# The last twenty entries of a hand-written emission list in another order, and one store moved behind them

## The chip, the cores and the metric

The kernel runs on one core of one Trainium2 chip. The metric is the device time of one execution in microseconds (us). The core has a matrix engine (TensorE, PE in the profile), which multiplies from on-chip memory (SBUF) into accumulators (PSUM), a vector engine (VectorE, DVE), an activation engine (ScalarE, ACT), a general engine (GpSimd, POOL), and SyncE (SP), which here issues nearly all DMA transfers, one after the other, from a queue of its own. Each engine works through its own list of instructions in order. An instruction that waits holds up everything behind it on that engine, and on SP that means the transfers behind it are not issued.

## The reference, cut to what matters

Three stages follow each other. The first is a delta-rule attention over 768 positions, the second a layer with a squared ReLU, the third a gated layer. The change touches the end of the second stage (called the first layer below) and the beginning of the preparation of the third (the second layer).

```python
def _moe_ref(x, w_in, w_out):            # x: 3072 x 384, w_in: 384 x 2048, w_out: 2048 x 384
    h = np.maximum(x @ w_in, 0.0)
    return (h * h @ w_out).astype(np.float32)

def _moe2_ref(x, w_gate, w_val, w_out):  # 384 -> 1536 -> 384
    gate = 1.0 / (1.0 + np.exp(-(x @ w_gate)))
    val = x @ w_val
    return (gate * val @ w_out).astype(np.float32)
```

The weights arrive as 64-bit numbers. The kernel turns them into 32-bit floats itself and keeps each as a high part and a low part, so that every product of the reference becomes three matrix multiplications (high with high, low with high, high with low).

## The kernel before, in words

The 3072 tokens are worked in six groups of 512 (`GT`), and the hidden width of the first layer in 16 slices of 128 (`NF1`). Piece n = 16 g + f, from 0 to 95, is slice f of group g. For each piece PE does nine multiplications for the hidden values (`h,n`, L677), and later nine for the output (`o,n`, L715), which add up in three PSUM tiles over the 16 slices of a group. Between the two, ACT takes the ReLU (L691) and squares it twice (L693, L694), and DVE makes the low part `gl` (`g,n`, L700). The hidden values live in two PSUM tiles (`ps_h`, tag `h`), so `h,n` cannot begin before the ReLU of `h,n-2` has been read.

The high parts of the weights stay in SBUF. The low parts are fetched from DRAM for each piece by SP at L655: `li,n` fetches the part that `h,n` needs, `lw,n` the part that `o,n` needs, each 192 KB, each into a ring of three tiles. All tiles of both rings have the name `il` in the profile.

The order of all this is written out by hand. `ORDER` is a list of entries such as `h,80` or `lw,82`, and the kernel emits the instructions of each entry in the order of the list (`run`, and `fns` for what a name stands for). The list ends with `h,81`. A loop then emits the remaining pieces in a regular pattern, one step for each piece n from 82 on: `h,n`, `li,n+2`, `lw,n+1`, `o,n-2`, `g,n`, and what `plan` holds for the step. So the first products behind the list are those of `h,82`, `o,80`, `h,83`, `o,81`. `plan` (filled by `at_step`) prepares the second layer: it loads the first layer's result back (`load_x2`, L887, at steps 1 and 2), converts the last third of the second layer's weights (`w2_late`, L786 to L807), and splits weights and inputs.

The first two thirds of the second layer's weights are converted within the list, in twelve chunks. `w2,i,k` is step k of chunk i: 0 fetches 768 KB (`raw`, L137, SP), 1 scales on ACT (L143), 2 and 3 are two DVE instructions each (L148 and L152, L157 and L161), 4 adds on POOL (L168), and 5 stores 384 KB to DRAM (`w2d`, L231, SP). Chunk 11 is the last.

Other entries in the stretch: `k2,5,1` fetches keys for the attention (L307, 384 KB in runs of 48 floats); of its possible readers, `s_piece` returns at once for group 5, half 1, so nothing reads this one. `x,5,1` splits the attention's result (L125 on ACT, L126 on DVE). `o,79` is the last piece of group 4, and ends with two copies on ACT (L726, L727) and one on DVE (L728); `po,4` stores them (L733, L734, SP).

```python
    with tc.manual_schedule():
        for token in ORDER.split():
            run(token)
```

Of the kernel before, what the change touches and what calls it, by code (L numbers as in the profile page):

```python
# [84 lines left out]
p,5,1 li,75 lw,73 lw,72 w,5,1 o,72 o,73 lw,74 g,74 v,5,1 w2,9,1 w2,9,2 sv,5,1 w2,9,3 s,5,0 li,78 h,75 z,5,0 g,75  # L85
w2,9,4 w2,9,5 h,76 g,76 o,74 ks,5,1 o,75 w2,10,0 w2,10,1 h,78 lw,76 x,5,0 li,77 t,5,1 o,76 h,77 g,77 y,5,1 li,82
li,79 lw,78 h,79 lw,77 lw,79 o,77 g,78 li,81 w2,10,2 z,5,1 w2,10,3 g,79 li,80 x,5,1 w2,10,4 w2,10,5 w2,11,0
w2,11,1 w2,11,2 w2,11,3 w2,11,4 k2,5,1 o,78 o,79 lw,82 h,80 lw,81 h,81 w2,11,5 g,80 li,83 po,4 g,81 lw,80
"""

@with_exitstack
def kernel(
# [132 lines left out]
    w2_todo = []  # L225
# [427 lines left out]
    def fetch_low(n, i):  # L653
        t = ring.tile([128, DM], F32R, tag=("il", "ol")[i], name="il", bufs=3)
        nc.sync.dma_start(out=t.bitcast(F32), in_=w1d[:, n % NF1, i])  # L655
        w1c[i, n] = t
# [10 lines left out]
    def moe1_hm(n, lo, hi_):  # L667
        g = n // NF1
        cs = slice(lo, hi_)
        if lo == 0:  # L670
            h_tile(n)
        hi, lo = w1h[n % NF1], w1c[0, n]
        xh, xl = xhi_t[g], xlo_t[g]
        ps = h_ps[n]
        for i, (w, x) in enumerate([(hi, xh), (lo, xh), (hi, xl)]):
            for kc in range(KD):
                nc.tensor.matmul(  # L677
                    out=ps[:, cs], lhsT=w[:, kc * 128:kc * 128 + 128], rhs=x[:, kc, cs],
                    start=(i == 0 and kc == 0), stop=(i == 2 and kc == KD - 1),
                )  # L680
# [22 lines left out]
    po = [None] * KD  # L703
# [35 lines left out]
    def keep_warm(n):  # L739
# [14 lines left out]
        k2=load_k2, kz=load_z, be=lambda: nc.sync.dma_start(out=beta_t, in_=beta), cs=constants, sq=squares, sm=sums, no=norms,  # L754
# [6 lines left out]
        w2=lambda i, k: w2_todo[i][k](), z=y_rows, po=put_x2,  # L761
        li=lambda n: fetch_low(n, 0), lw=lambda n: fetch_low(n, 1), h=moe1_h, h0=lambda n: moe1_hm(n, 0, GT // 2),
# [7 lines left out]
    with tc.manual_schedule():  # L770
# [115 lines left out]
        def load_x2(g):  # L886
            nc.sync.dma_start(out=x2r_t[:, g % 2], in_=x2d[g])  # L887
# [52 lines left out]
        def at_step(n, *fns):  # L940
            plan.setdefault(n, []).extend(fns)

        at_step(1, lambda: load_x2(0))
        at_step(2, lambda: load_x2(1))
        for m in range(NW):
# [348 lines left out]
```

## Time and profile before

| | us |
|---|---|
| median of three runs | 1089.73 (1089.73 to 1089.91) |
| the profiled execution, its own time | 1089.84 |
| its span (first to last instruction) | 1088.1 |
| PE busy | 1013.5 (93%) |
| DVE busy | 765.8 (70%) |
| ACT busy | 462.5 (43%) |
| POOL busy | 200.1 (18%) |
| longest wait of PE on a transfer (L715 for `il`) | 6.4 |

PE is busy for 93% of the span, and the chain of work that ended last runs through PE for 84% of it. So a wait of PE is what to look for, and what such a wait costs is read in the stretch where it stands. A row of the timeline gives the start and the duration of an instruction, or of several equal ones together, and in brackets how long its engine had been idle and for what. The durations of matrix multiplications overlap, so the distance from one start to the next is the measure of PE's pace.

### The profile page before, as it was taken

To read this page: it belongs to the slowest core of one execution; us is meant where nothing else is said; L and a number is where in the kernel's file an instruction comes from. 1 tells how busy PE (TensorE), PEld (TensorE's weight loads), DVE (VectorE), ACT (ScalarE), POOL (GpSimd) and SP (SyncE) were. 2 spreads that over 40 slices of the span, in tenths; PEclk is the share of its full clock that TensorE was granted. 3 is DMA by queue.
4 is the path that set the end of the run, shared out by engine and by line. 5 is a ranking of instruction groups with operands and counts; after the bars stand their busy time and mean duration, and the time that the engine had idled before them with its cause. 6 is when DMAs were issued, how large, how long until landed. Compare 5 with 4: busy or idle time off the path is not lost.

```text
span 1088.1 us, 27387 instructions
## 1 busy us (share of the span) xinstructions
PE 1013.5 (93%) x11611; PEld 830.8 (76%) x11611; DVE 765.8 (70%) x1450; ACT 462.5 (43%) x762; POOL 200.1 (18%) x157
## 2 busy tenths in 40 slices
PE   3476999999998999999996999999999999999998
PEld 2475778877887888888785887777888888878878
DVE  6779879868777776875342498888776665686770
ACT  2253765454454455445543574434332232233220
POOL 4342444100001101010010122335401221000000
PEclk9998999999999999999998999999999999999999
DMA  9766756775685956575545867553545323244302
GB/s 241 198 198 177 223 180 196 217 205 147 175 201 163 234 164 206 168 176 166 144 151 164 277 187 277 189 198 117 189 156 160 106 93 125 87 128 154 125 3 57
DMA packets 104843, 182.78 MB, mean 168 GB/s; under 512 B 46608, under 2 KB 79504, under 8 KB 100112
## 3 DMA queue, kind: packets, MB, share of 16 engines
q1 hardware_dynamic: 104432, 180.76, 55.7%
q8 instruction: 91, 1.49, 0.6%
q10 hardware_dynamic: 288, 0.26, 0.1%
q14 instruction: 32, 0.26, 0.1%
HBM read 139.30 MB, written 36.96 MB: 162 GB/s over the span
## 4 chain that ended last, share of the span: by engine, by line
PE 84%; DVE 8%; issue 4%; DMA 2%; ACT 1%; POOL 1%; SPq 1%; DVEq 0%; ACTq 0%; POOLq 0%
PE o L715 18%; PE h L677 18%; PE gx L1135 11%; PE gy L1135 11%; PE o L1014 10%; PE r L1194 2%; PE att L594 2%; PE att L536 1%; PE att L551 1%; PE att L582 1%; PE att L363 1%; PE att L616 1%; PE att L564 1%; PE att L377 1%; PE att L618 1%
## 5 line engine op out<-in xcount | busy, mean ns | idle before, releaser
L700 DVE TENSOR_TENSOR gl<-gg,gh 128x512 fp32r<-128x512 f32 x96 | 73.8, 776 | 106.6 <-ACT gg L694 106.5
L691 ACT ACTIVATE gg<-h 128x512 f32<-128x512 f32 x96 | 57.5, 598 | 190.0 <-PE h L677 181.2
L715 PE MATMUL o<-gh,il 128*128 128x512 f32 x288 | 113.9, 395 | 6.4 <-DMA il<-w1d 6.4
L1014 PE MATMUL o<-gh,wo 128*128 128x512 f32 x270 | 93.0, 394 | 0.0
L715 PE MATMUL o<-gh,w1h 128*128 128x512 f32 x216 | 88.1, 408 | 0.0
L715 PE MATMUL o<-gl,w1h 128*128 128x512 f32 x216 | 85.5, 396 | 0.0
L677 PE MATMUL h<-xhi,il 128*128 128x512 f32 x288 | 82.6, 395 | 0.9 <-issue 0.8
L1135 PE MATMUL gx<-xa,wg 128*128 128x512 f32 x288 | 76.7, 395 | 2.1 <-DVE valB L1047 1.2
L1135 PE MATMUL gy<-xa,wg 128*128 128x512 f32 x288 | 76.2, 393 | 0.0
L715 PEld LDWEIGHTS o<-gh,il 128*128 128x128 f32 x288 | 54.9, 191 | 17.5 <-DMA il<-w1d 6.8
L677 PE MATMUL h<-xhi,w1h 128*128 128x512 f32 x216 | 65.6, 413 | 1.8 <-ACT gg L691 1.8
L1135 PEld LDWEIGHTS gx<-xa,wg 128*128 128x128 f32 x288 | 53.6, 188 | 16.4 <-DVE gateB L1047 2.3
L677 PEld LDWEIGHTS h<-xhi,il 128*128 128x128 f32 x288 | 54.8, 191 | 13.7 <-issue 1.0
L1135 PEld LDWEIGHTS gy<-xa,wg 128*128 128x128 f32 x288 | 53.7, 188 | 13.0 <-DVE gateC L1047 0.4
L694 ACT ACTIVATE gg<-gg 128x512 f32<-128x512 f32 x96 | 60.7, 632 | 3.1
L693 ACT ACTIVATE gh<-gg 128x512 fp32r<-128x512 f32 x96 | 60.7, 632 | 3.1
L677 PE MATMUL h<-xlo,w1h 128*128 128x512 f32 x216 | 61.9, 396 | 0.0
L1014 PEld LDWEIGHTS o<-gh,wo 128*128 128x128 f32 x270 | 50.7, 188 | 11.9
L168 POOL TENSOR_TENSOR y<-raw 128x768 f32<-128x768 f32 x12 | 18.8, 1566 | 216.6 <-DVE raw L161 184.7
L1014 PE MATMUL o<-gl,wo 128*128 128x512 f32 x135 | 53.2, 394 | 0.0
L461 DVE TENSOR_TENSOR tmp<-xi,tt 128x40 f32<-128x40 f32 (+7 forms) x208 | 52.2, 284 | 1.2
L468 DVE TENSOR_TENSOR tt<-tt,tmp 128x40 f32<-128x40 f32 (+7 forms) x208 | 50.5, 276 | 1.4
(228 smaller groups left out, 2264.5 us busy)
## 6 DMA issues: line engine op xcount, KB each, us to landing
il<-w1d SPq DMA_DIRECT2D x192, 192.0 KB, 3.7
wg<-wgd SPq DMA_DIRECT2D x24, 1152.0 KB, 5.2
raw<-in_w_dram SPq DMA_DIRECT2D x19, 768.0 KB, 5.1
wgd<-wg SPq DMA_DIRECT2D x12, 1152.0 KB, 6.0
w1s<-in_w_dram SPq DMA_DIRECT2D x9, 768.0 KB, 5.3
w1d<-wl SPq DMA_DIRECT2D x16, 384.0 KB, 4.0
kz<-in_kz_dram SPq DMA_DIRECT2D x32, 192.0 KB, 5.1
kn<-in_kn_dram SPq DMA_DIRECT2D x12, 384.0 KB, 4.6
```

The source lines that it names most:

```text
L461: nc.vector.tensor_tensor(out=tv[i], in0=xi[:, 0:j, j].unsqueeze(2).to_broadcast([128, j, n]), in1=tt[:, j, lo:hi].unsqueeze(1).to_broadca ...
L468: nc.vector.tensor_tensor(out=tt[:, 0:j, lo:hi], in0=tt[:, 0:j, lo:hi], in1=tv[i], op=ALU.subtract)
L594: nc.tensor.matmul(out=psv[c][tok(a), k, :], lhsT=k2_t[st][tok(a), 8 * c + k, :], rhs=u_t[st][tok(a), 8 * c + k, 0:HD], start=True, stop=True,
L677: nc.tensor.matmul(out=ps[:, cs], lhsT=w[:, kc * 128:kc * 128 + 128], rhs=x[:, kc, cs], start=(i == 0 and kc == 0), stop=(i == 2 and kc == ...
L691: nc.scalar.activation(out=gg, in_=ps, func=ACTF.Relu)
L693: nc.scalar.activation(out=gh, in_=gg, func=ACTF.Square)
L694: nc.scalar.activation(out=gg, in_=gg, func=ACTF.Square)
L700: nc.vector.tensor_tensor(out=gl, in0=gg, in1=gh.bitcast(F32), op=ALU.subtract)
L715: nc.tensor.matmul(out=po[m], lhsT=w[:, cs], rhs=x, start=(f == 0 and i == 0), stop=(f == NF1 - 1 and i == 2),)
L1014: nc.tensor.matmul(out=po2[g, m], lhsT=w, rhs=x, start=start, stop=stop)
L1135: nc.tensor.matmul(out=ps, lhsT=a, rhs=c, start=k == 0 and u == us[0], stop=k == 2 and u == us[-1],)
L1194: nc.tensor.matmul(out=po_m, lhsT=x[:, cs], rhs=w, start=f == 0 and i == 0, stop=f == NF2 - 1 and i == 2)
```

## The change

The last twenty entries of the list stand in another order, and one of them, `w2,11,5` (the store of the last chunk), has left the list: it is issued in step 2 of the loop, before the second load of the first layer's result. Nothing is computed in another way.

```diff
@@ -85,7 +85,7 @@
 li,79 lw,78 h,79 lw,77 lw,79 o,77 g,78 li,81 w2,10,2 z,5,1 w2,10,3 g,79 li,80 x,5,1 w2,10,4 w2,10,5 w2,11,0
-w2,11,1 w2,11,2 w2,11,3 w2,11,4 k2,5,1 o,78 o,79 lw,82 h,80 lw,81 h,81 w2,11,5 g,80 li,83 po,4 g,81 lw,80
+lw,80 o,78 lw,81 o,79 k2,5,1 h,80 lw,82 h,81 g,80 li,83 w2,11,1 w2,11,2 g,81 w2,11,3 w2,11,4 po,4
 """
@@ -940,6 +940,7 @@
         def at_step(n, *fns):
             plan.setdefault(n, []).extend(fns)
 
+        at_step(2, lambda: w2_todo[11][5]())
         at_step(1, lambda: load_x2(0))
         at_step(2, lambda: load_x2(1))
```

PE's own order is the same in both kernels. On SP, before, from the fetch of the last chunk (`raw`) on; `il_8434` is `lw,82`, `il_8451` is `lw,81`, `il_8471` is `li,83`, `il_8477` is `lw,80`:

```order
L137 DMA raw_8401<-in_w2_dram 128x1536
L307 DMA k21_119<-in_ks_dram 128x16x48
L655 DMA il_8434<-w1d_105 128x384
L655 DMA il_8451<-w1d_105 128x384
L231 DMA w2d_106<-y_8404 128x768
L655 DMA il_8471<-w1d_105 128x384
L733 DMA x2d4_70<-o01_8429 128x1024
L734 DMA x2d4_70<-o2_8430 128x512
L655 DMA il_8477<-w1d_105 128x384
```

The same place on SP after the change; here `il_8403` is `lw,80`, `il_8414` is `lw,81`, `il_8446` is `lw,82`, `il_8465` is `li,83`:

```order
L137 DMA raw_8401<-in_w2_dram 128x1536
L655 DMA il_8403<-w1d_105 128x384
L655 DMA il_8414<-w1d_105 128x384
L307 DMA k21_119<-in_ks_dram 128x16x48
L655 DMA il_8446<-w1d_105 128x384
L655 DMA il_8465<-w1d_105 128x384
L733 DMA x2d4_70<-o01_8425 128x1024
L734 DMA x2d4_70<-o2_8426 128x512
```

`lw,80` has moved from behind the store and `po,4` to the place right behind the fetch of `raw`, and the store (L231) is gone from here. On SP it stands now further down, in the loop, between the fetches of `li,86` and `lw,85` (`il_8570`, `il_8572`) and the second load of the first layer's result (`x2d1`):

```order
L887 DMA x2r_8486<-x2d0_66 128x1536
L655 DMA il_8570<-w1d_105 128x384
L655 DMA il_8572<-w1d_105 128x384
L231 DMA w2d_106<-y_8468 128x768
L887 DMA x2r_8486<-x2d1_67 128x1536
L786 DMA raw2_8488<-in_w2_dram 128x768
```

On ACT, before, from the split of the attention's result on (the three rows from L691 are the ReLU and the squares of `h,80`, the next of `h,81`):

```order
L125 CAST xhi<-xr 128x3x256
L143 ACTIVATE raw<-raw 128x768
L726 COPY o_8429<-o_7360 128x512
L727 COPY o_8429<-o_7361 128x512
L691 ACTIVATE gg<-h 128x512
L693 ACTIVATE gh<-gg 128x512
L694 ACTIVATE gg<-gg 128x512
```

And after the change:

```order
L125 CAST xhi<-xr 128x3x256
L726 COPY o_8425<-o_7360 128x512
L727 COPY o_8425<-o_7361 128x512
L691 ACTIVATE gg<-h 128x512
L693 ACTIVATE gh<-gg 128x512
L694 ACTIVATE gg<-gg 128x512
L691 ACTIVATE gg<-h 128x512
L693 ACTIVATE gh<-gg 128x512
L694 ACTIVATE gg<-gg 128x512
L143 ACTIVATE raw<-raw 128x768
```

The scaling of the chunk (L143), which waits for the fetch of `raw`, has moved from ahead of the copies and of the ReLUs of `h,80` and `h,81` to behind them.

## Rows read from the trace of the kernel before

**Rows 1.** Page, first line: the span.
```profile
span 1088.1 us, 27387 instructions
```
**Rows 2.** Timeline of PE, 573 to 610: start, duration, instruction, count, idle before.
```profile
573.50 0.84 PE L677 MATMUL h<-xhi,w1h 128*128 128x512 f32 x3
575.54 0.84 PE L677 MATMUL h<-xhi,w1h 128*128 128x512 f32 x3
...
579.50 0.97 PE L677 MATMUL h<-xhi,w1h 128*128 128x512 f32 x3 [1.76 <-ACT gg L691]
...
581.68 0.39 PE L715 MATMUL o<-gh,w1h 128*128 128x512 f32 x1
588.48 0.79 PE L715 MATMUL o<-gh,il 128*128 128x512 f32 x1 [6.41 <-DMA il<-w1d]
...
594.84 0.40 PE L715 MATMUL o<-gh,w1h 128*128 128x512 f32 x1
...
609.14 0.84 PE L677 MATMUL h<-xhi,w1h 128*128 128x512 f32 x3
```
**Rows 3.** Windows: stretch, length, busy us of five engines, clock, DMA share, GB/s.
```profile
579.50:581.68 2.18, 2.18 (x10) 1.80 (x10) 2.11 (x4) 2.12 (x4) 0.37 (x1) 1.00 0.03 11
581.68:588.48 6.80, 0.39 (x3) 0.01 (x1) 2.94 (x4) 2.74 (x5) 1.09 (x1) 0.87 0.72 256
588.48:592.05 3.57, 3.57 (x8) 2.80 (x9) 0.00 (x0) 0.00 (x0) 0.00 (x0) 0.50 0.02 8
```
**Rows 4.** Timeline of SP's queue, 572 to 603: start, time to issue, transfer.
```profile
572.01 0.38 SPq L137 DMA_DIRECT2D raw<-in_w_dram  x1
572.44 0.55 SPq L307 DMA_DIRECT2D k<-in_ks_dram  x1
573.08 3.74 SPq L655 DMA_DIRECT2D il<-w1d  x1
...
582.80 0.32 SPq L231 DMA_DIRECT2D w2d<-y  x1
...
584.72 1.01 SPq L655 DMA_DIRECT2D il<-w1d  x1
...
601.31 0.43 SPq L887 DMA_DIRECT2D x2r<-x2d  x1
...
602.26 0.43 SPq L655 DMA_DIRECT2D il<-w1d  x1
```
**Rows 5.** DMA issues at 572.01, 572.44, 573.08, 584.72, 602.26: size, us to landing.
```profile
raw<-in_w_dram SPq DMA_DIRECT2D x1, 768.0 KB, 5.0
k<-in_ks_dram SPq DMA_DIRECT2D x1, 384.0 KB, 6.9
...
il<-w1d SPq DMA_DIRECT2D x1, 192.0 KB, 6.8
...
il<-w1d SPq DMA_DIRECT2D x1, 192.0 KB, 3.7
...
il<-w1d SPq DMA_DIRECT2D x1, 192.0 KB, 5.4
```
**Rows 6.** Timeline of ACT, 577 to 579.
```profile
577.12 0.88 ACT L143 ACTIVATE raw<-raw 128x768 f32<-128x768 f32 x1 [4.72 <-DMA raw<-in_w_dram]
...
578.84 0.61 ACT L691 ACTIVATE gg<-h 128x512 f32<-128x512 f32 x1
```
**Rows 7.** Instructions on tile raw, 560 to 590: duration ns min/median/max.
```profile
L148 DVE TENSOR_SCALAR y<-raw x2: 554/558/562, 566.5 to 578.0; 128x768 uint32<-128x768 uint32 x2
...
L161 DVE SCALAR_TENSOR_TENSOR raw<-raw,y x2: 959/960/960, 568.6 to 580.2; 128x768 f32<-128x768 uint32 x2
L168 POOL TENSOR_TENSOR y<-raw x2: 1467/1652/1837, 569.7 to 581.3; 128x768 f32<-128x768 f32 x2
```
**Rows 8.** Waits of PE, 594 to the end: total us, times, longest.
```profile
PE gx L1135 <- DVE valC L1047: 1.6, 1, 1.6
```

## The prediction

> **What bounds the kernel now.** I read the page first, then PE's own timeline around the changed entries, then what released its waits (SP's queue, the landings of its transfers, ACT), and last the granted clock of the same stretch. The profiled execution took 1089.84 us, 1.74 more than its span [rows 1] and 0.11 more than the median of the runs.
>
> PE should be followed from `h,80` on, where the changed entries begin to matter. `h,80` starts at 573.50 and `h,81` at 575.54 [rows 2], so a piece of nine multiplications takes 2.04 us at full pace, 0.227 each. `h,82` would follow at 577.58, but starts at 579.50: it needs the PSUM tile of `h,80`, and ACT reads that only at 578.84, because it had first waited for the fetch of `raw` until 577.12 and then scaled it and made two copies [rows 6]. `o,80` begins at 581.68 and stops after one product: the second, which needs `lw,80`, comes at 588.48 after 6.41 us of idleness [rows 2]. `lw,80` is the transfer issued at 584.72 [rows 4], landing 3.7 later at 588.4 [rows 5]. It was issued so late because the store of the last chunk stood before it on SP, and that was issued at 582.80 only [rows 4], when POOL had finished the chunk. The chain is thus: fetch of `raw`, ACT, four DVE instructions, POOL, store, and only then a weight that PE needs at once.
>
> [...] `o,81` starts at 594.84 [rows 2].
>
> **What the change takes away.** `lw,80` moves ahead of the store, and the store leaves this place; L143 moves behind the activations of `h,80` and `h,81`. PE's order does not change. From 573.50 to 594.84 there are 21.34 us with five pieces (`h,80`, `h,81`, `h,82`, `o,80`, `h,83`), 45 products, which at full pace take 5 x 2.04 = 10.20. The 11.14 us between are, by the starts in [rows 2]:
> - `h,82` late, 579.50 - 577.58 = 1.92;
> - its own piece, 2.18 instead of 2.04: 0.14;
> - `o,80` between its first and second product, 6.80 instead of 0.23: 6.57;
> - the 17 products from 588.48 to 594.84, 6.36 instead of 17 x 0.227 = 3.86: 2.50, the price of the slow clock.
>
> Sum 11.13. If nothing new is late, `h,82` starts at 577.58, `o,80` at 579.62, `h,83` at 581.66, `o,81` at 583.70, and all that follows on PE comes 11.1 us earlier.
>
> [...] The rows show 0.50 after the idle time, and 1.00 in 579.50 to 581.68, after the shorter wait of 1.76 [rows 2, 3]. [...]
>
> **What could be late next, step by step.**
> - `lw,80` is needed by the second product of `o,80`, at 579.85. It is now issued where the keys were, at 572.44 [rows 4]. The fetch of `raw` ahead of it lands at 572.01 + 5.0 = 577.0. A 192 KB part lands 0.5 behind its predecessor when the queue is full: `k` at 572.44 + 6.9 = 579.3, the `il` behind it at 573.08 + 6.8 = 579.9 [rows 4, 5]. So `lw,80` lands at 577.5, and cannot be later than the 579.9 of that `il`, which had both ahead of it: the cost lies between 0 and 0.1. I take 0.
> - `lw,81` follows 0.5 later, at 578.0, and is needed at 583.9.
> - `li,83` is needed by the fourth product of `h,83`, at 581.66 + 0.68 = 582.3. Ahead of it now stand `raw`, `lw,80`, `lw,81`, `k` and `lw,82`. `k` took 2.3 behind `raw` (577.0 to 579.3), so 577.0 + 2 x 0.5 + 2.3 + 2 x 0.5 = 581.3. SP must also get to issue it. Behind `k`, the issue of one `il` took 3.74, to 576.82 [rows 4], 2.5 before `k` landed; with `k` 1.0 later this ends at 577.8, and `li,83` is issued at about 577.9, 3.4 before the landing worked out. The margin is 1.0, the smallest here. Cost between 0 and, if SP were held until `k` has landed (580.3) and the transfer then took the 3.7 of the one at 584.72 [rows 5], 584.4 - 582.3 = 2.1. I take 0, since the only row of this situation says so.
> - ACT: the copies no longer wait for `raw`, so the ReLU of `h,80` is at 575.7 and its PSUM tile free at 576.3, before 577.58. L143 now comes behind six activations of about 0.6 [rows 6], at 579.7, when `raw` has long landed, and ends at 580.6. The ReLU of `h,82`, ready at 579.8, is 0.8 late; its result is wanted by `o,82` at 587.8. Hidden by two pieces and more.
> - DVE: `gl` of piece 81 now stands behind L148 and L152. From 580.6: 0.56 [rows 7], another of 0.96 like L161 [rows 7], and a `gl` of some 0.7 give 582.9; `o,81` wants it with its third product, at 584.2. Margin 1.3, cost 0; without that cover each us of delay on ACT is one of PE.
> - POOL and the store: the remaining two DVE instructions end at 584.4, POOL adds up to 1.84 [rows 7]: 586.2. SP comes to the store just before the second load of the first layer's result, which it issued at 601.31 [rows 4], now at 601.31 - 11.1 = 590.2. No wait, by 4 us. It costs SP some 0.4 and the queue 384 KB, at the pace of the `il` (192 KB in 0.5) 1.0. Behind it stands `li,87`: issued at 602.26, landed 5.4 later at 607.7 [rows 4, 5], needed by the fourth product of `h,87`, at 609.14 + 0.68 = 609.8 [rows 2]. Of the 2.1 us 0.7 to 1.1 remain. Cost 0; with the store at half that pace (2.0 and 0.4) 0.3.
>
> So the sum is -11.1: 1089.84 - 11.1 = 1078.7, and against the median, which lies 0.11 below, 1078.6. Downstream PE waits only for DVE's part of the second layer [rows 8], which follows PE itself; I let 1.0 to either side stand for these handovers, less than the longest of them.
>
> **The rivals.**
> 1. *The wait moves to the next fetch* (`li,83` at `h,83`, or `li,87` behind the store). For it: the margins of 1.0 and 0.7; 3.74 us for an issue behind `k`. Against it: the same row, carried over, still leaves the margin. Price: up to 2.1 for `li,83` and 0.3 for `li,87`, and half a us for a restart like those 0.14; no slow clock, as after the 1.76 [rows 3]. Together 1079.2 to 1081.3. Chance 0.2.
> 2. *The clock does not come back*: the terms of waiting go (8.6), the 2.50 stay. For it: 0.87 was already granted within the stretch with the wait [rows 3]. Against: 1.00 before it. 1089.73 - 8.6 = 1081.1. Chance 0.04.
> 3. *The change doesn't do what it says*: `lw,80` is emitted before `o,78`, and if its tile came free only behind `o,79` and the landing slipped again behind other transfers, the hole at `o,80` would stay. Against: `lw,82` stood in that very place and was issued at 573.08 [rows 4]. Time 1089.7, if all of it stayed. Chance 0.03.
> 4. *Slower*: the store as a plug on SP. In the loop every fetch of PE stands behind it. If POOL finished the chunk late, SP would hold `x2d1`'s load, the second layer's first slab and `li,87` together. It decides from POOL's end at 590.2 + 0.7 = 590.9 on; to eat 11.1 us, of which 2.5 would be a slow clock again, POOL would have to end near 599.5, and 3 us later the time is 1092.7. For it: that queue did just this at 582.80. Against: POOL's end at 586.2 by the rows. Chance 0.02.
>
> **How the numbers follow.** The forecast has 0.71. Its own range is 1077.6 to 1079.6 by the handovers. The range goes to 1077.2 below and 1081.6 above, which takes in rivals 1 and 2 and leaves out 3, 4 and a forecast that is off for a reason not listed here. A measurement can tell 0.2%, 2.2 us, from no change; the forecast and rivals 1 and 2 are faster by more, 0.95, of which I give 0.01 away to what is not listed; no change 0.03; slower 0.03.
>
> **What the profile after would show.** Right: no idle time of PE before L677 or L715 between `h,80` and `o,81`, the granted clock at 1.00 through the whole stretch, nine products every 2.04; the `il` behind `raw` landing about 0.5 after it; L143 without idle time before it; the store's issue without a wait, just before the second load. Wrong: an idle time of PE for `il` at the fourth product of a piece of `h` (rival 1), 0.50 in the clock without a wait before it (rival 2), a hole after the first product of `o,80` (rival 3), SP's queue waiting for POOL at L231 in the loop (rival 4). A span under 1075 would mean that something behind `o,81` gained too.

## The result and the profile after

The changed kernel took 1077.71 us (median of 4 runs, 1074.27 to 1079.54) beside 1089.82 for the kernel before: ratio 0.988, 95% interval 0.985 to 0.9911. In a second series it took 1075.98 (6 runs) beside 1088.0 (29 runs, 1083.02 to 1095.11): 0.9888, 0.9856 to 0.9921. The first median lies 0.9 below the forecast. The second lies below the range, and so does 0.988 x 1089.73 = 1076.7. The profiled execution took 1074.27; the first line of its page, which answers to [rows 1]:

```profile
span 1072.5 us, 27390 instructions
```

PE's timeline of the changed kernel, from `h,80` to `o,81` and at `h,87`, answers to [rows 2]:

```profile
568.39 0.84 PE L677 MATMUL h<-xhi,w1h 128*128 128x512 f32 x3
...
570.43 0.84 PE L677 MATMUL h<-xhi,w1h 128*128 128x512 f32 x3
...
572.48 0.84 PE L677 MATMUL h<-xhi,w1h 128*128 128x512 f32 x3
...
574.51 0.39 PE L715 MATMUL o<-gh,w1h 128*128 128x512 f32 x1
574.74 0.39 PE L715 MATMUL o<-gh,il 128*128 128x512 f32 x1
...
576.55 0.84 PE L677 MATMUL h<-xhi,w1h 128*128 128x512 f32 x3
...
578.60 0.39 PE L715 MATMUL o<-gh,w1h 128*128 128x512 f32 x1
...
592.88 0.84 PE L677 MATMUL h<-xhi,w1h 128*128 128x512 f32 x3
594.12 0.96 PE L677 MATMUL h<-xhi,il 128*128 128x512 f32 x3 [0.41 <-DMA il<-w1d]
```

Three things are to be seen. The pieces follow each other every 2.04 us; the wait ahead of `h,82` and the hole behind the first product of `o,80` are gone, and `h,80` to `o,81` takes 578.60 - 568.39 = 10.21 instead of 21.34. A new wait stands at `h,87`: its `il` products come 1.24 behind its start instead of 0.68. And `h,80` itself starts 5.1 us earlier than before, although PE's instructions ahead of it are the same and the order on the other engines differs only within the last 1.5 us before it.

The windows of the changed kernel (stretch, length, busy us of PE, PEld, DVE, ACT and POOL, clock, DMA share, GB/s) show a clock of 1.00 from `h,80` to `h,87`, where [rows 3] had 0.50 from 588.48 to 592.05:

```profile
568.39:578.60 10.21, 10.21 (x47) 8.45 (x46) 4.51 (x7) 6.37 (x11) 0.00 (x0) 1.00 1.07 313
578.60:592.88 14.28, 14.28 (x65) 11.83 (x64) 3.17 (x5) 7.37 (x12) 1.79 (x1) 1.00 0.74 259
```

SP's queue of the changed kernel (start, time to issue, transfer), beside [rows 4]:

```profile
566.90 0.38 SPq L137 DMA_DIRECT2D raw<-in_w_dram  x1
567.38 0.48 SPq L655 DMA_DIRECT2D il<-w1d  x1
...
568.95 4.06 SPq L655 DMA_DIRECT2D il<-w1d  x1
573.12 0.37 SPq L655 DMA_DIRECT2D il<-w1d  x1
...
585.10 0.38 SPq L231 DMA_DIRECT2D w2d<-y  x1
585.53 0.42 SPq L887 DMA_DIRECT2D x2r<-x2d  x1
...
586.64 0.51 SPq L655 DMA_DIRECT2D il<-w1d  x1
```

The landings of those issued at 566.90 (`raw`), 567.38 (`lw,80`), 573.12 (`li,83`), 585.53 (the second load of the first layer's result) and 586.64 (`li,87`), with size and us to landing, beside [rows 5]:

```profile
raw<-in_w_dram SPq DMA_DIRECT2D x1, 768.0 KB, 5.2
...
il<-w1d SPq DMA_DIRECT2D x1, 192.0 KB, 5.3
...
il<-w1d SPq DMA_DIRECT2D x1, 192.0 KB, 3.4
...
x2r<-x2d SPq DMA_DIRECT2D x1, 768.0 KB, 7.1
...
il<-w1d SPq DMA_DIRECT2D x1, 192.0 KB, 7.4
```

`raw` lands at 572.1. `lw,80` lands at 572.7 and is needed at 574.74. `li,83` lands at 576.5 and is needed at 576.55 + 0.68 = 577.23. `li,87` lands at 594.1 and is needed at 593.56: that is the new wait. The store at 585.10 did not wait for POOL, whose last addition begins at 579.17 and takes 1.79; L143 on ACT has no idle time before it any more, in contrast to [rows 6]:

```profile
579.17 1.79 POOL L168 TENSOR_TENSOR y<-raw 128x768 f32<-128x768 f32 x1 [12.71 <-DVE raw L161]
```

```profile
574.51 0.87 ACT L143 ACTIVATE raw<-raw 128x768 f32<-128x768 f32 x1
```

PE's waits from 568 to the end, the groups of `gx` by valC (the same as in [rows 8], one line lower in the file) and of `h`:

```profile
PE gx L1136 <- DVE valC L1048: 1.6, 1, 1.6
...
PE h L677 <- DMA il<-w1d: 0.4, 1, 0.4
```

So one execution can be cut at three marks: the start of `h,80`, `o,81`, and the first `gx` product. From there to the end every kernel here took 438.0 to 438.2. The table gives the marks of one profile of each kernel. Its last columns are the ratio that follows from the two middle stretches alone (their sum against the 76.44 of before, over 1088), and the measured one:

```
kernel                 h,80    h,80-o,81  o,81-gx  by the marks  measured
before                 573.50  21.34      55.10
before, repeated       573.34  21.27      55.08    0.9999        1.0008 [0.9979, 1.0037]
changed                568.39  10.21      55.78    0.9904        0.988  [0.985, 0.9911]
changed, repeated      566.31  10.20      55.82    0.9904        0.9888 [0.9856, 0.9921]
lw,80 early only       567.06  14.19      55.09    0.9934        0.994  [0.9914, 0.9966]
conversion late only   574.67  23.54      55.08    1.0020        1.0035 [1.0008, 1.0062]
store in the list      575.77  10.20      63.02    0.9970        0.9975 [0.9952, 0.9998]
before, PE kept busy   569.82  19.00      55.08    0.9978        0.9979 [0.9949, 1.0009]
store at step 9        568.53  10.20      55.08    0.9897        0.9885 [0.9855, 0.9916]
the same without k2    569.73  10.20      55.08    0.9897        0.9897 [0.9863, 0.9931]
```

Each ratio worked out from the marks lies in the measured interval. The gain of the change is 10.4 to 10.5 us, 11.1 in the list less 0.7 at `h,87`. The start of `h,80`, with the same instructions of PE ahead of it in every kernel, scatters over 9.5 us.

### The profile page after: what moved, and what is told of

It reads as the page before. It is cut to its first block, busy times and chain, and to the rows that moved or that the text cites. A ratio compares the mean times of both kernels' runs of the same rounds, so it can differ in the third digit from the quotient of the medians.

```text
span 1072.5 us, 27390 instructions
## 1 busy us (share of the span) xinstructions
PE 1008.8 (94%) x11611; PEld 828.3 (77%) x11611; DVE 763.4 (71%) x1450; ACT 462.4 (43%) x762; POOL 201.4 (19%) x157
## 4 chain that ended last, share of the span: by engine, by line
PE 85%; DVE 7%; issue 3%; DMA 2%; ACT 1%; SPq 1%; POOL 1%; DVEq 0%; ACTq 0%; POOLq 0%
PE h L677 18%; PE o L715 18%; PE gx L1136 12%; PE gy L1136 11%; PE o L1015 10%; PE r L1195 2%; PE att L594 2%; PE att L536 1%; PE att L363 1%; PE att L551 1%; PE att L582 1%; PE att L616 1%; PE att L564 1%; DMA il<-w1d 1%; PE att L618 1%
## 5 line engine op out<-in xcount | busy, mean ns | idle before, releaser
L700 DVE TENSOR_TENSOR gl<-gg,gh 128x512 fp32r<-128x512 f32 x96 | 70.3, 738 | 96.4 <-ACT gg L694 96.2
L691 ACT ACTIVATE gg<-h 128x512 f32<-128x512 f32 x96 | 57.4, 598 | 185.7 <-PE h L677 175.1
L715 PEld LDWEIGHTS o<-gh,il 128*128 128x128 f32 x288 | 54.1, 188 | 10.5
L168 POOL TENSOR_TENSOR y<-raw 128x768 f32<-128x768 f32 x12 | 19.1, 1593 | 221.0 <-DVE raw L161 221.0
```

Source lines behind the costliest of these rows:

```text
L691: nc.scalar.activation(out=gg, in_=ps, func=ACTF.Relu)
L700: nc.vector.tensor_tensor(out=gl, in0=gg, in1=gh.bitcast(F32), op=ALU.subtract)
L715: nc.tensor.matmul(out=po[m], lhsT=w[:, cs], rhs=x, start=(f == 0 and i == 0), stop=(f == NF1 - 1 and i == 2),)
```

## The experiments

**The two kernels again.** No edit.

> The kernel before once more, unchanged. Marks are read from PE's timeline: the start of h,80 (573.50 in the first trace of before, 568.39 in that of the changed kernel, though every instruction ahead of it is the same in both), and the distance from there to the start of o,81 (21.34 and 10.21). Theory A: the 5.1 us by which the changed kernel reached h,80 earlier are scatter of the first 150 us (attention start-up), which differs from execution to execution; then this second trace of the same program may reach h,80 anywhere from 568 to 575, and its times scatter by some 3 to 5 us around 1089. Theory B: the lead belongs to the changed program; then this one reaches h,80 at 573.5 within 0.5 and its times stay within 1 us of 1089.8. Both: 21.3 from h,80 to o,81.

> The changed kernel once more, unchanged. Theory A (start-up scatter): h,80 starts anywhere from 568 to 575, the times spread from 1074 to 1080 and sit 10.6 below those of before on average (11.1 from h,80 to o,81, less the 0.6 that h,87 now waits for li,87). Theory B (the lead belongs to the program): h,80 at 568.4 within 0.5, median near 1074.5. Both: 10.2 from h,80 to o,81, and a wait of h,87 for il of 0.3 to 0.7.

Measured: 1088.62 (12 runs, 1081.7 to 1096.8) and 1075.98 (6 runs, 1072.25 to 1077.6). The middle stretches repeat to 0.1 us. The three runs of before that lay within 0.18 of each other had understated the scatter: the same kernel ranges over 15 us.

**Only `lw,80` early.** The list of before with one entry moved; the store stays where it was, and L143 too.

```
- w2,11,4 k2,5,1 o,78 o,79 lw,82 ... po,4 g,81 lw,80
+ w2,11,4 lw,80 k2,5,1 o,78 o,79 lw,82 ... po,4 g,81
```

> The kernel before with one entry moved: lw,80 stands ahead of k2,5,1, the rest of the list as before (the scaling of the last chunk ahead of the copies, the store at its old place in the list). My theory, by terms: the hole in o,80 (6.57) and the slow clock behind it (2.50) go, h,82's 2.06 stay; but li,83 is still behind the store (issued at 583.2 on the scale of before, landed at 585.9) while h,83 wants it at 584.4, so 1.5 of it comes back as a wait of h,83: 14 us from h,80 to o,81, a gain of 7 to 7.5. Rival: the late activation (L143 ahead of the ReLUs) is what matters, and lw,80 alone gives under 4.

Measured: ratio 0.994, `h,80` to `o,81` 14.19. PE's timeline of this kernel, and the window from `h,82` to the second product of `o,80`:

```profile
573.23 1.04 PE L677 MATMUL h<-xhi,w1h 128*128 128x512 f32 x3 [1.93 <-ACT gg L691]
...
576.63 0.63 PE L715 MATMUL o<-gh,w1h 128*128 128x512 f32 x1
577.05 0.55 PE L715 MATMUL o<-gh,il 128*128 128x512 f32 x1
```

```profile
573.23:577.05 3.82, 3.82 (x10) 2.99 (x11) 3.75 (x6) 2.98 (x5) 1.46 (x1) 0.60 0.09 31
```

The hole at `o,80` is gone (0.42 from its first product to its second), the wait at `h,82` stays, and now the clock falls to 0.60 behind that wait of 1.93: `h,82` takes 3.40 instead of 2.04. This part alone brings 7.2 us of the 11.1. The 14 us that were expected came out, but by luck: the wait of 1.5 forecast for `h,83` did not come. Its `il` products start at 579.76, 0.70 behind its first product, and the trace gives no wait ahead of them. `h,83` is late itself by then: 579.76 is 12.70 behind `h,80`, where the landing that the expectation took, 585.9 on the scale of before, is 12.4 behind. The slow clock in `h,82`, 1.36 us that the expectation did not have, stands in its place.

**Only the conversion later.** The last conversion's steps and its store move behind `g,80` and `li,83`, and `lw,80` stays last, behind the store. (The line below shows that the change reorders the last seventeen entries of the list, not twenty.)

```
- w2,11,1 w2,11,2 w2,11,3 w2,11,4 k2,5,1 o,78 o,79 lw,82 h,80 lw,81 h,81 w2,11,5 g,80 li,83 po,4 g,81 lw,80
+ k2,5,1 o,78 o,79 lw,82 h,80 lw,81 h,81 g,80 li,83 w2,11,1 w2,11,2 g,81 w2,11,3 w2,11,4 w2,11,5 po,4 lw,80
```

> The kernel before with the other half of the change: the last chunk's ACT, DVE and POOL steps stand as in the changed list, behind h,81 and g,80, but the store stays in the list behind them, and lw,80 behind the store. My theory: h,82 no longer waits (2.06 gained), but POOL now ends 3.4 to 5 later than in before, and the store, po,4 and lw,80 with it; lw,80 lands near 591 on the scale of before, o,80 stands still from 579.9 to about 591.5, and the slow clock comes as before. 23 to 25 us from h,80 to o,81 against 21.3: slower than before by 2 to 4. Rival: L143's place is what cost before, so this is faster than before by 2 or more.

Measured: ratio 1.0035, `h,80` to `o,81` 23.54. PE's timeline of this kernel:

```profile
580.79 0.39 PE L715 MATMUL o<-gh,w1h 128*128 128x512 f32 x1
592.69 0.80 PE L715 MATMUL o<-gh,il 128*128 128x512 f32 x1 [11.51 <-DMA il<-w1d]
```

`h,82` is in time, since `o,80` stands 6.12 behind `h,80`. But the chunk's steps stand later in this list, the store behind them, and `lw,80` behind the store: the hole grows from 6.41 to 11.51. This half of the change alone makes the kernel slower, by 2.2 us between the marks. The two edits are worth more together than apart: as long as `lw,80` stands behind the store, PE only waits longer at `o,80` for what it no longer waits at `h,82`, and the second product of `o,80` starts 592.69 - 574.67 = 18.02 behind `h,80` instead of 588.48 - 573.50 = 14.98.

**The store as an entry of the list.** The changed kernel with the store back in its list, ahead of `po,4`:

```
- g,81 w2,11,3 w2,11,4 po,4
+ g,81 w2,11,3 w2,11,4 w2,11,5 po,4
- at_step(2, lambda: w2_todo[11][5]())
```

> The changed list, but the store of the last chunk is an entry again, behind the last conversion step and ahead of po,4, instead of a call in the loop. On SP it then stands right behind li,83, and po,4 and the il of h,84 stand behind it. Theory (the place of the store is half of the change): h,80 to o,81 stays at 10.2 us, but the store waits on SP for POOL until about 581.0 (by the clock of the changed kernel's profile, 12.6 after h,80), so li,84 is issued near 582.2 instead of 574.54 and lands near 586; the fourth product of h,84, at 581.32 in the changed kernel, waits some 4.5 us, and more if the granted clock falls after it. o,81 to the first gx: 55.8 + 4 to 7 = 60 to 63 us, h,80 to the end 508 to 511 instead of 504.1. Rival (the store costs no more on SP than where it is now): o,81 to the first gx at 55.1 to 55.8. For the stretch ahead of h,80, whose instructions are the same in every kernel: if its time only scatters from one execution to the next, h,80 starts anywhere from 566 to 575; if it hangs on the kernel, at 566 to 568 as in the three kernels that fetch lw,80 early.

Measured: ratio 0.9975, `h,80` to `o,81` 10.20, `o,81` to `gx` 63.02. SP's queue, PE's timeline and a window of this kernel:

```profile
588.36 0.32 SPq L231 DMA_DIRECT2D w2d<-y  x1
...
589.76 2.41 SPq L655 DMA_DIRECT2D il<-w1d  x3
```

```profile
588.01 0.84 PE L677 MATMUL h<-xhi,w1h 128*128 128x512 f32 x3
593.78 1.65 PE L677 MATMUL h<-xhi,il 128*128 128x512 f32 x3 [4.93 <-DMA il<-w1d]
```

```profile
596.50:599.99 3.49, 3.49 (x10) 2.72 (x9) 0.69 (x1) 1.86 (x3) 0.00 (x0) 0.56 0.59 214
```

The store is issued 588.36 - 575.77 = 12.59 behind `h,80` (POOL ends 12.57 behind it in the changed kernel). From 576.34 + 4.11 = 580.45, where the issue of `li,83` ended, to 588.36 SP issues nothing, and `li,84` stands behind the store for these 7.9 us. PE loses 4.93 and then a stretch at a clock of 0.56. So 7.2 us of the gain (63.02 - 55.78) hang on the one line that takes the store out of the list. This is the mechanism of the prediction's rival 4, at the place where it does happen. `h,80` starts at 575.77, the latest of all, with `lw,80` early: an early start does not come with that order.

**Before, with PE kept busy through its idle time.** The kernel before, with 30 dummy products behind `h,82`, whose results nothing reads:

```
  moe1_h(n)
+ if n == N1 - NF1 + 2:
+     keep_warm(30)
```

> The kernel before with 30 dummy products put behind h,82, into the PSUM tile that h,82 has yet to hand over, so that TensorE works on through the idle time ahead of the second product of o,80; they add work whose results nothing reads. Theory (the slow clock after the idle time is a term of 2.5 us by itself): the second product of o,80 comes no earlier than before, 15.0 us after h,80, but the products after it run at 0.227 us each and a granted clock near 1.0, so h,80 to o,81 is 21.34 - 2.3 = 18.9 to 19.3. Rival (the clock falls there for another reason than the idle time): 21.3, at 0.50 behind it. If h,80's own place only scatters it lies between 566 and 575; if it hangs on the kernel, at 573 to 575 as in the three kernels with the old place of lw,80.

Measured: ratio 0.9979, `h,80` to `o,81` 19.00. PE's timeline of this kernel, and the window behind the dummies:

```profile
577.94 6.96 PE L750 MATMUL h<-w1h 128*128 128x512 f32 x30
584.74 0.39 PE L715 MATMUL o<-gh,w1h 128*128 128x512 f32 x1
584.96 0.39 PE L715 MATMUL o<-gh,il 128*128 128x512 f32 x1
```

```profile
584.97:588.82 3.85, 3.85 (x19) 3.19 (x17) 0.00 (x0) 0.00 (x0) 0.00 (x0) 1.00 0.26 85
```

The second product starts as late as before, 15.14 behind `h,80` (before 14.98). But behind it the clock is 1.00, and the 17 products from there to `o,81` take 588.82 - 584.96 = 3.86 instead of 6.36: 2.50 us are won by that alone. The whole stretch gains 21.34 - 19.00 = 2.34, because the second product itself came 0.16 later. By the interval this kernel is not told from before; the row of the window shows the clock, 1.00 where it was 0.50 and then 0.73 before (588.48 to 592.05 and 592.05 to 594.84). `h,80` starts at 569.82 here, with the list of before, so the old order has no late `h,80` of its own either.

**The store at step 9.** The changed kernel, with the store seven steps later in the loop:

```
- at_step(2, lambda: w2_todo[11][5]())
+ at_step(9, lambda: w2_todo[11][5]())
```

> The changed kernel with the store of the last chunk at step 9 of the second layer's preparation instead of step 2. Theory (the store ahead of the second load of the first layer's result makes that load and li,87 behind it land late): without it there x2r1 lands some 4.4 us after its issue instead of 7.1, li,87 in time, no wait of the il products in h,87, and o,81 to the first gx is 55.1 instead of 55.8; h,80 to o,81 stays 10.2. So 0.6 us less than the changed kernel, which is less than the scatter of a run and shows in the marks of the trace alone. Rival (the wait of h,87 comes from the slab load or the first load that stand there too): 55.8 again, or the wait moves to the fetch behind step 9. For h,80's own place: 566 to 575 if it scatters, 566 to 568 if it hangs on the kernel.

Measured: 1076.21, ratio 0.9885; `o,81` to `gx` 55.08. The landings of the second load and of `li,87` (issued at 585.18 and 586.13), and `h,87` on PE:

```profile
x2r<-x2d SPq DMA_DIRECT2D x1, 768.0 KB, 4.6
...
il<-w1d SPq DMA_DIRECT2D x1, 192.0 KB, 5.1
```

```profile
593.01 0.84 PE L677 MATMUL h<-xhi,w1h 128*128 128x512 f32 x3
593.69 0.84 PE L677 MATMUL h<-xhi,il 128*128 128x512 f32 x3
```

No wait; the load lands 4.6 after its issue instead of 7.1. The 0.7 us at `h,87` are the store's. No time can show that: 1076.21 against 1075.98 and 1077.71 is scatter.

**The same without the last keys.** The fetch `k2,5,1` of 128 pieces of 16x48 dropped as well; no later instruction reads its tile, so no part of the result is left out.

```
- lw,80 o,78 lw,81 o,79 k2,5,1 h,80 lw,82
+ lw,80 o,78 lw,81 o,79 h,80 lw,82
```

> As the kernel with the store at step 9, and the fetch of the last 128x16x48 block of keys is left out (its place in the list is dropped; nothing later reads it in this list's remainder, the operations on it stay out). Theory (the issue of 4.06 us of the il behind it, and the late landing, come from this fetch of short pieces): lw,82 is issued in about 0.4 us, li,83 about 3.5 us earlier, and lands about 2.3 us earlier against h,80 (some 5.9 us after h,80 instead of 8.1), so its margin at h,83 grows from 0.7 to about 3; the time doesn't change, h,80 to o,81 10.2, o,81 to gx as with the keys. Rival (SP's issue is held by the queue as such): an issue of 3 to 4 us stays, one or two places further. For h,80's own place: 566 to 575 if it scatters, 566 to 568 if it hangs on the kernel.

Measured: 1076.4, ratio 0.9897, `h,80` to `o,81` 10.20, `o,81` to `gx` 55.08. SP's queue of this kernel, `lw,81` and `lw,82` together, then `li,83`:

```profile
569.29 0.95 SPq L655 DMA_DIRECT2D il<-w1d  x2
```

```profile
571.29 0.32 SPq L655 DMA_DIRECT2D il<-w1d  x1
```

The issue of 4.06 is gone, so it came from the keys. `li,83` lands 4.0 after 571.29, at 575.3, and is needed at 578.57: the margin is 3.3 instead of 0.7. The time doesn't change, as a margin is not a wait.

## Why the prediction was right, and where it failed

**The gain in the list** was forecast as 11.13 and measured as 21.34 - 10.21 = 11.13. Each of its terms went: `h,82` starts 2.05 behind `h,81`, the second product of `o,80` 0.23 behind the first, and the clock is 1.00. The two holes were taken away one at a time by the kernels above, and the price of the slow clock, 2.50 by the sum, is 6.36 - 3.86 = 2.50 in the run with the dummies. The sum let the 2.50 go with the idle time. That was my estimate from 0.50 behind the wait of 6.41 and 1.00 behind that of 1.76 [rows 2, 3]; no run of the time showed it. In the run with the dummies, with work in the idle time, the clock is 1.00 from `h,82` to `o,81`, and in the changed kernel, without the idle time, it is 1.00 too: at this place the slow stretch goes with the idle time.

**The covers**, against the start of `h,80`: `lw,80` lands 0.5 behind `raw`, as forecast. `li,83` lands 8.1 behind (forecast 7.8) and is needed 8.85 behind (8.8), so the margin was 0.7 and not 1.0. L143 starts 6.1 behind (6.2), `gl` of piece 81 is ready 9.2 behind (9.4), POOL ends 12.57 behind (12.7), and the store is issued 16.71 behind (16.7). All of them held.

**The store ahead of `li,87`** is the term of the sum that was mis-sized, and rival 1 named its place: "Of the 2.1 us 0.7 to 1.1 remain. Cost 0; with the store at half that pace (2.0 and 0.4) 0.3." I had priced 384 KB written as if they were an `il` read, 1.0 and 0.4 of issue. Against the kernel with the store at step 9, `li,87` lands 25.69 behind `h,80` instead of 22.74: 2.95 later, twice what I took. With 2.42 of margin there, 0.53 is waited, and with the restart (these `il` products take 594.92 - 594.12 = 0.80 instead of 0.68) 0.70 is lost. So rival 1 came true in part, at a price of 0.70 instead of 0.3. (Its bounds, 1079.2 to 1081.3, don't follow from its own prices: 0.3 + 0.5 and 2.1 + 0.3 + 0.5 on 1078.6 give 1079.4 and 1081.5, still inside the range.)

**The step that failed** is the base and its spread: "1089.84 - 11.1 = 1078.7, and against the median, which lies 0.11 below, 1078.6", with "1.0 to either side" for handovers only. It has no term for the stretch ahead of `h,80`, and so takes its time as a constant, from three runs that lay within 0.18 of each other. The sentence "A span under 1075 would mean that something behind `o,81` gained too" fell with it: the span is 1072.5, behind `o,81` 0.7 was lost, and the 5.1 came from ahead of `h,80`. PE's timelines of before and of the changed kernel show that most of this is there by 240 us, at the same product of the attention, 4.3 apart (the count of 22 ends with the window, at 242.5):

```profile
241.80 0.95 PE L363 MATMUL att<-kt 48*64 48x64 f32 x22 [1.54 <-issue]
```

```profile
237.51 1.84 PE L363 MATMUL att<-kt 48*64 48x64 f32 x63 [2.71 <-issue]
```

With a base of 1088.0 to 1088.5 (medians of 29 and of 23 runs) and the 10.45 of the marks, 1077.6 to 1078.0 comes out. That is nearly the forecast, because the base was 1.2 to 1.7 too high and the 0.7 at `h,87` left out, errors of opposite signs; that the first median lies only 0.9 from the forecast is in part luck. The ten runs of the changed kernel have a median of 1076.4, some 1.4 lower, which the scatter can hold. A median less its two middle stretches leaves 1009.96 to 1014.00 in the kernels with `lw,80` early, and 1011.27 to 1014.47 in those with its old place: the two overlap for the most part, and by estimate from these remainders a range of 2 to 3 us to either side would have been due.

**What stays open** is why the stretch ahead of `h,80` scatters. After the first six profiles one could suspect that the kernels with `lw,80` early also start `h,80` early (566 to 568, the others 573 to 575); 575.77 in one of these and 569.82 with the old list speak against it. The windows from 40 us to `h,80`, before and changed, show that it is not waiting alone:

```profile
40.00:573.50 533.50, 502.08 (x8975) 416.03 (x8975) 386.89 (x830) 271.19 (x441) 100.06 (x64) 0.98 0.65 184
```

```profile
40.00:568.39 528.39, 500.14 (x8977) 415.15 (x8975) 385.62 (x830) 271.87 (x443) 101.08 (x64) 0.99 0.66 186
```

Of the 5.1 us, 31.42 - 28.25 = 3.2 are idle time of PE, and 502.08 - 500.14 = 1.9 are more busy time on the same products. In the kernel with the store in the list, from 40 us to its `h,80` at 575.77, the busy time is 505.09. The idle time is made of many waits: those for DVE sum to 11.1 in both, those whose releaser the trace gives as "issue" to 19.1 before and 15.1 after the change. None of the runs changes one of them, so the cause is not shown.

## What to carry to other kernels

Cut the trace at marks behind which all executions agree, and compare stretches: here they repeat to 0.1 us where whole runs scatter by 15. A store that waits for a chain of engines belongs on a queue behind the fetches that PE needs next, not ahead of them (ahead of them it cost 7.2 us), and it should be priced apart from loads (this one delayed a landing by 2.95 where 1.4 was taken). Three times within 0.18 are no measure of the scatter, so a base needs a range of its own.

## What the runs showed of the hardware that was not expected

- A store of 384 KB ahead of a load of 768 KB made that load take 7.1 us from its issue to its landing instead of 4.6, and the fetch two places behind it land 2.95 later.
- The issue of a fetch behind the 128x16x48 keys took 4.06 (3.74 in [rows 4]); without the keys two such issues took 0.95 together.
- The clock fell to 0.60 behind a wait of 1.93 in the kernel with only `lw,80` early, and stayed at 1.00 behind one of 1.76 before [rows 3] and one of 1.70 in the kernel with the dummies (575.76 to 584.97). Rival 1 of the prediction had counted on no slow clock behind so short a wait; why these differ is not shown.
- In the profile of the kernel with the store in the list the granted clock was 0.50 between 40 and 60 us. The window beside that of the kernel before, the same columns as above:

```profile
40.00:60.00 20.00, 12.97 (x425) 12.17 (x425) 13.07 (x21) 9.48 (x16) 9.93 (x6) 0.50 0.68 231
```

```profile
40.00:60.00 20.00, 12.97 (x425) 12.18 (x425) 12.53 (x20) 9.32 (x16) 9.92 (x6) 1.00 0.67 209
```

The same 425 products in the same 12.97 us, at half the clock: for these small products of the attention it cost nothing in this stretch, where 17 products of 512 columns lost 2.50 to it. (No product of 512 columns stands in these 20 us, so the 0.50 there is the profile's record alone.)
